# Output weights of a gated layer split into two parts where they are rounded, gate rows copied by one queue, last output products by token rows

## Chip, core and metric

The kernel runs on one core of a Trainium2 chip. The metric is the device time of one execution in microseconds (us); smaller is better. The core has five engines that work from their own instruction queues, in order: PE (TensorE, matrix products; PEld is its weight load), DVE (VectorE), ACT (ScalarE), POOL (GpSimd) and SP (SyncE, which only issues transfers). Transfers (DMAs) are issued from the queues of SP, ACT and POOL and carried by the same 16 DMA engines.

## The reference

```
X = rfft(x, axis=1);  y = irfft(X * (filt_r + 1j*filt_i))        # 8 batches, 3072 tokens, 256 wide
logits = y @ phi                                                 # 32 slots, 4 for each of 8 experts
slots  = softmax(logits over tokens).T @ y
slots  = relu(slots @ w1[e]) @ w2[e]                             # each expert on its own 4 slots
z = softmax(logits over slots) @ slots                           # back to 24576 tokens
out = (silu(z @ w_gate) * (z @ w_val)) @ w_out                   # 256 -> 1536 -> 256
```

## The kernel before

The work has three stages. **The first** (`phase1`) does the Fourier transforms as matrix products in 96 units, six for each of 16 half batches. A unit is written out by hand: load x (`load_x`, two transfers), products X with the transform (L258), multiplication by the filter on DVE and POOL (P, Q, yt), transposes T (L283) into a single buffer of PSUM, which ACT copies to `y` (L284), products with phi, and now and then a piece of the chain for the logits of an earlier batch (`chain`; its `dd` is computed by ACT at L428 and L435 and multiplied by PE at L443; its `lgd` are four transfers of logits to DRAM, L404).

Beside this runs a generator, `conv`, one step in the middle and one at the end of every unit. It rounds w_gate, w_val and w_out in 36 chunks of 128 x 256 numbers, chunks 24 to 35 being w_out. The four steps of a chunk are: ACT makes `mag` (L579); ACT makes `low` and the sign (L581, L582); DVE shifts `mag` (L584); POOL adds and multiplies into `low` (L586, L588), SP writes the result from `low` to DRAM (`wod` for w_out, L589) and loads the raw numbers (`raw`) of the chunk after next (L566). `mag`, `low` and `raw` have two buffers each, so chunk n+2 writes into the buffers of chunk n.

**The second** (`transition`) runs the experts on the 32 slots and multiplies the result by w_gate and w_val. So z never has to be formed: each token's 32 softmax weights times these rows (`g4`, `v4`, three tiles of 512 columns each) give gate and value. The rows are kept as a rounded part and the rest. Tile 0 is made in place; tiles 1 and 2 are copied there row by row with 16 transfers from `gh` and `gl` (L887), half of them on SP's queue and half on POOL's.

**The third** (`phase2`) goes over 576 items (batch, third, half, column block f of 12). For an item, `gv` makes G and V on PE (L980, L981) and silu on ACT (L983), `gate` the product h on DVE (L989), `split` a rounded part `hi` (ACT, L996) and the rest `lo` (DVE, L997), and three or four items later `proj` multiplies these by w_out on PE (L1008, L1012) into four accumulators, one for each block of 128 tokens (t). After the last f, ACT copies half of an accumulator (L1021), DVE adds the other half (L1022), and SP writes four transfers to `out`. w_out is loaded once in its second place (`wo`, index 1) by SP at the start of this stage, and `load_out` splits a block of it in each of the first twelve items: ACT rounds into index 0 (L969), POOL subtracts (L970).

Of the kernel before, what the change touches and what calls it, by code (L numbers as in the profile page):

```python
# [7 lines left out]
F32 = mybir.dt.float32  # L8
F32R = mybir.dt.float32r
# [3 lines left out]
ALU = mybir.AluOpType  # L13
# [4 lines left out]
NB, SEQ, D, E = 8, 3072, 256, 32  # L18
NEXP, SPE, FE, FF = 8, 4, 1024, 1536
NJ, NP, NR = 24, 96, 32  # L20
NF = FF // 128
# [58 lines left out]
def spectral_softmoe_glu_kernel(  # L80
# [17 lines left out]
    nc = tc.nc  # L98
    pe, dve, act, pool = nc.tensor, nc.vector, nc.scalar, nc.gpsimd

    dram = ctx.enter_context(tc.tile_pool(name="dram", bufs=1, space=DRAM))
# [8 lines left out]
    sb_ = const.tile([32, NB], F32, name="sb_")  # L110
    sp = const.tile([128, D], F32, name="sp")
    expo = const.tile([128, 1], F32, name="expo")
    wd = [dram.tile([256, FF], F32, name="wgd"), dram.tile([256, FF], F32, name="wvd"), dram.tile([FF, 256], F32, name="wod")]
    sld = dram.tile([128, NB - 2, D], F32, name="sld")
    cd = dram.tile([2, 3, E, 1024], F32, name="cd")
    lgd = [dram.tile([NP, 2, E, 16], F32, name=f"lgd{b}") for b in range(NB)]
# [20 lines left out]
    def phase1():  # L137
        with ExitStack() as c1:
# [412 lines left out]
            def flat(a):  # L551
                return a.rearrange("(p a) f -> p (a f)", p=128)

            def conv():


                cw = 256
                chunks = [(i, c) for i in range(3) for c in range(FF * D // 128 // cw)]
                raws = {}

                def load(n):
                    if n >= len(chunks):
                        return
                    i, c = chunks[n]
                    raws[n] = cvp.tile([128, cw, 2], I32, tag="raw", name="raw", bufs=2)
                    nc.sync.dma_start(  # L566
                        out=raws[n].rearrange("p n k -> p (n k)"),
                        in_=flat((w_gate, w_val, w_out)[i])[:, c * cw:(c + 1) * cw].bitcast(I32),
                    )

                load(0)
                load(1)
                yield
                for n, (i, c) in enumerate(chunks):
                    raw = raws.pop(n)
                    hf, lw = raw[:, :, 1].bitcast(F32), raw[:, :, 0].bitcast(U32)
                    mag = cvp.tile([128, cw], I32, tag="mag", name="mag", bufs=2)
                    low = cvp.tile([128, cw], I32, tag="low", name="low", bufs=2)
                    act.activation(mag.bitcast(F32), hf, AF.Copy, scale=2.0 ** -112)  # L579
                    yield  # L580
                    act.activation(low, lw, AF.Copy, scale=2.0 ** -29)  # L581
                    act.activation(hf, hf, AF.Sign)  # L582
                    yield
                    dve.tensor_scalar(mag, mag, 3, None, ALU.logical_shift_left)  # L584
                    yield
                    pool.tensor_tensor(out=low, in0=mag, in1=low, op=ALU.add)  # L586
                    mf = low.bitcast(F32)
                    pool.tensor_tensor(out=mf, in0=mf, in1=hf, op=ALU.mult)  # L588
                    nc.sync.dma_start(out=flat(wd[i])[:, c * cw:(c + 1) * cw], in_=mf)  # L589
                    load(n + 2)  # L590
                    yield

            def first_weights():

# [51 lines left out]
            for k in range(2):  # L646
# [4 lines left out]
                out=nyq, in_=bass.AP(filt_r.tensor, SEQ // 2 * D, [[1, 128], [128, 2]])  # L651
# [10 lines left out]
            todo = []  # L662
# [87 lines left out]
    def transition():  # L750
# [110 lines left out]
        for w, dst in gates:  # L861
            pg = bank([128, 512], "h")
            for d_ in range(2):
                pe.matmul(
                    out=pg, lhsT=sot[:, d_, :], rhs=w[:, d_, 0:512], start=(d_ == 0), stop=(d_ == 1)
# [7 lines left out]
        for d_ in range(2):  # L873
            for i, (w, n, c) in enumerate(parts):
                pe.matmul(
                    out=pg[32 * i:32 * i + 32, :],
                    lhsT=sot[:, d_, 0:32],
                    rhs=w[:, d_, c * 512:(c + 1) * 512],
                    start=(d_ == 0),
                    stop=(d_ == 1),  # L880
# [3 lines left out]
        dve.tensor_tensor(out=gl, in0=pg, in1=gh, op=ALU.subtract)  # L884
        for i, (w, n, c) in enumerate(parts):
            for r in range(4):
                (nc.sync if r < 2 else nc.gpsimd).dma_start(  # L887
                    out=later[n][c][32 * r:32 * r + 32, :].bitcast(F32),
                    in_=(gl if r % 2 else gh)[32 * i:32 * i + 32, :].bitcast(F32),
                )  # L890
# [4 lines left out]
    def phase2_tiles():  # L895
# [3 lines left out]
        wo4 = [cp.tile([128, 4, 2, D], F32R, name=f"wo{c}") for c in range(3)]  # L899
        wo = [wo4[f // 4][:, f % 4] for f in range(NF)]  # L900
        c4 = {}

        def first():
            t = cp.tile([128, 3, 2, 512], F32R, tag="c4", name="c4", bufs=2)

            for r in range(4):
                (nc.sync if r < 2 else nc.scalar).dma_start(
                    out=t[32 * r:32 * r + 32].rearrange("p q G n -> p q (G n)").bitcast(F32),
                    in_=cd[r // 2].rearrange("q e n -> e q n"),
                )  # L910
            c4[0] = t
            for c in range(3):
                nc.sync.dma_start(
                    out=wo4[c][:, :, 1, :].bitcast(F32),
                    in_=wd[2][c * 512:(c + 1) * 512, :].rearrange("(f p) d -> p f d", p=128),
                )

        def build(b):
# [42 lines left out]
    def phase2(later):  # L961
        cp, g4, v4, wo, c4, build = (later[k] for k in ("cp", "g4", "v4", "wo", "c4", "build"))
        kp = p2.enter_context(tc.tile_pool(name="kp", bufs=3))
        ps_g = p2.enter_context(tc.tile_pool(name="ps_g", bufs=2, space=PSUM))
        ps_o = p2.enter_context(tc.tile_pool(name="ps_o", bufs=1, space=PSUM))

        def load_out(f):
            st = wo[f][:, 1, :].bitcast(F32)
            act.copy(wo[f][:, 0, :], st)  # L969
            pool.tensor_tensor(out=wo[f][:, 1, :], in0=st, in1=wo[f][:, 0, :], op=ALU.subtract)  # L970

        items = [(b, q, G, f) for b in range(NB) for q in range(3) for G in range(2) for f in range(NF)]
        hb, hhi, hlo, acc, sb2 = {}, {}, {}, {}, {}

# [17 lines left out]
        def split(i):  # L992
# [4 lines left out]
            dve.tensor_tensor(out=lo, in0=h, in1=hi, op=ALU.subtract)  # L997
            hhi[i], hlo[i] = hi, lo

        def proj(i):  # L1000
            b, q, G, f = items[i]
            hi, lo = hhi.pop(i), hlo.pop(i)
            if f == 0:
                acc[0] = [ps_o.tile([128, 512], F32, tag=f"o{t}", name=f"o{t}") for t in range(4)]
            for t in range(4):
                a = acc[0][t]
                ts = slice(128 * t, 128 * t + 128)
                pe.matmul(  # L1008
                    out=a, lhsT=hi[:, ts], rhs=wo[f].rearrange("p k d -> p (k d)"),
                    start=(f == 0), stop=(f == NF - 1), skip_group_check=True,  # L1010
                )
                pe.matmul(  # L1012
                    out=a[:, D:2 * D], lhsT=lo[:, ts], rhs=wo[f][:, 0, :],
                    start=False, stop=(f == NF - 1), skip_group_check=True,
                )
            if f == NF - 1:
                ot = kp.tile([128, 4, D], F32, tag="ot", name="ot", bufs=2)
                for t in range(4):
                    a = acc[0][t]
                    tmp = kp.tile([128, D], F32, tag="tmp", name="tmp", bufs=4)  # L1020
                    act.copy(tmp, a[:, D:2 * D])  # L1021
                    dve.tensor_tensor(out=ot[:, t, :], in0=a[:, 0:D], in1=tmp, op=ALU.add)  # L1022
                row = b * SEQ + 1024 * q + 16 * G
                for ii in range(4):
                    nc.sync.dma_start(
                        out=bass.AP(out.tensor, (row + 4 * ii) * D, [[32 * D, 32], [1, 4 * D]]),
                        in_=ot[32 * ii:32 * ii + 32].rearrange("p t d -> p (t d)"),
                    )

        def lag(i):  # L1030

            r = i % (6 * NF) - EXP_AT
            if r in (1, 2, 3, 4, 5, 6):
                return (4, 3, 3, 3, 4, 4)[r - 1] if i < len(items) - 6 * NF else LAG
            return min(LAG, 3 + i // 10)

        todo = list(range(len(items)))
        gen = build(1)
        for i in range(len(items) + LAG):
            if i < len(items):  # L1040
                b, q, G, f = items[i]
                if q == 0 and G == 0 and f == 0 and b:
                    for _ in gen:
                        pass
                    gen = build(b + 1) if b + 1 < NB else iter(())
                gv(i)
            while todo and todo[0] <= i - lag(i):
                proj(todo.pop(0))
            if i < len(items):
                gate(i)  # L1050
            if i < NF:
                load_out(i)
            if 0 <= i - 1 < len(items):
                split(i - 1)
            if i % 4 == 1 and i > NF:
                next(gen, None)

    with tc.manual_schedule():
        phase1()
        phase2(transition())  # L1060
        p2.close()
# [32 lines left out]
```

## Time and profile before

| | |
|---|---|
| median of 3 runs (lowest to highest) | 1496.86 us (1495.06 to 1497.08) |
| the profiled execution: its time, its span | 1496.74 us, 1495.0 us |
| busy: PE, DVE, ACT, POOL | 96%, 78%, 64%, 16% of the span |
| chain that ended last, by engine | PE 85%, DVE 7%, DMA 3%, ACT 2% |
| first stage, second stage, third stage | to about 381, to about 407, to the end |

The span is that from the first to the last instruction of the profiled execution; 1.74 us of its time lie around it. "Busy" is time in which the engine executes. The chain that ended last is followed back from the last instruction, at each step to what released it.

### The profile page before, as it was taken

How to read it: one execution, taken by the hardware profiler on the slowest of the kernel's cores; microseconds unless marked ns; L12 is line 12 of the kernel's file. 1: busy time of each engine (PE TensorE's matmuls, PEld its weight loads, DVE VectorE, ACT ScalarE, POOL GpSimd, SP SyncE). 2: the span in 40 equal slices, each digit the busy share in tenths (PEclk: the TensorE clock that was granted, in tenths of full speed). 3: DMA queues.
4: the chain of work that ended last, by engine and by line, in shares of the span. 5: the costliest groups of instructions: out<-in, count | busy, mean ns of one | idle time of the engine just before them, and what ended most of it. 6: DMA issues, size and time to landing. Idle time of an engine off the chain costs nothing.

```text
span 1495.0 us, 25170 instructions
## 1 busy us (share of the span) xinstructions
PE 1440.3 (96%) x9562; PEld 1152.0 (77%) x9562; DVE 1163.0 (78%) x1894; ACT 961.1 (64%) x1837; POOL 243.5 (16%) x315
## 2 busy tenths in 40 slices
PE   4899899998899999999999999999999999999998
PEld 2566566665488888888888888888888888888887
DVE  2788888876378878878887887888789778877775
ACT  2476566663367667666766766676676667666665
POOL 0466666653020000000000000000000000000000
PEclk9999999999999999999999999999999999999999
DMA  9968877868710220220131112112110210211011
GB/s 226 156 118 160 154 131 148 167 153 339 277 44 14 51 60 15 50 60 16 28 71 27 27 36 54 36 29 48 48 29 20 66 39 23 49 43 25 19 29 29
DMA packets 87848, 116.42 MB, mean 78 GB/s; under 512 B 8880, under 2 KB 65072, under 8 KB 87600
## 3 DMA queue, kind: packets, MB, share of 16 engines
q1 hardware_dynamic: 80480, 102.37, 31.3%
q10 hardware_dynamic: 6800, 11.54, 2.5%
q8 instruction: 75, 1.23, 0.4%
q0 software_dynamic: 448, 0.92, 0.2%
q14 instruction: 45, 0.37, 0.1%
HBM read 68.13 MB, written 34.60 MB: 69 GB/s over the span
## 4 chain that ended last, share of the span: by engine, by line
PE 85%; DVE 7%; DMA 3%; ACT 2%; issue 1%; POOL 1%; SPq 0%; ACTq 0%; DVEq 0%; POOLq 0%
PE o L1008 35%; PE o L1012 18%; PE V L981 9%; PE G L980 9%; PE X L258 4%; PE s L230 2%; DVE sg L238 2%; PE T L283 2%; DVE P L262 1%; DVE Q L263 1%; PE c L477 1%; DMA fraw<-in_filt_i_dram 1%; PE L L291 1%; DMA raw<-in_moe_w_out_dram 1%; ACT b L247 1%
## 5 line engine op out<-in xcount | busy, mean ns | idle before, releaser
L1008 PE MATMUL o<-wo,hi 128*128 128x512 f32 x2304 | 833.1, 396 | 2.7 <-POOL wo L970 2.7
L1012 PE MATMUL o<-wo,lo 128*128 128x256 f32 x2304 | 645.3, 280 | 0.0
L983 ACT ACTIVATE s<-G 128x512 f32<-128x512 f32 x576 | 345.2, 599 | 322.7 <-PE G L980 319.4
L989 DVE TENSOR_TENSOR h<-V,s 128x512 f32<-128x512 f32 x576 | 395.0, 686 | 171.6 <-ACT s L983 170.8
L1008 PEld LDWEIGHTS o<-wo,hi 128*128 128x128 f32 x2304 | 432.9, 188 | 106.8 <-POOL wo L970 3.0
L1012 PEld LDWEIGHTS o<-wo,lo 128*128 128x128 f32 x2304 | 434.6, 189 | 25.3
L997 DVE TENSOR_TENSOR lo<-h,hi 128x512 fp32r<-128x512 f32 x576 | 422.4, 733 | 1.1
L996 ACT CAST hi<-h 128x512 fp32r<-128x512 f32 x576 | 354.7, 616 | 11.5 <-DVE h L989 8.2
L981 PE MATMUL V<-c,v 128*128 128x512 f32 x576 | 227.7, 395 | 1.1 <-DVE h L989 1.1
L980 PE MATMUL G<-c,g 128*128 128x512 f32 x576 | 228.3, 396 | 0.2 <-ACT s L983 0.2
L258 PEld LDWEIGHTS X<-fwd,b 128*128 128x128 f32 x768 | 95.6, 196 | 58.4 <-issue 41.0
L980 PEld LDWEIGHTS G<-c,g 128*128 128x128 f32 x576 | 108.2, 188 | 26.2 <-ACT s L983 0.9
L238 DVE STREAM_TRANSPOSE sg<-s 128x1024 f32<-128x1024 f32 x64 | 79.2, 1240 | 55.4 <-PE s L230 53.8
L258 PE MATMUL X<-fwd,b 128*128 128x128 f32 x768 | 112.0, 290 | 2.5 <-ACT b L247 1.3
L981 PEld LDWEIGHTS V<-c,v 128*128 128x128 f32 x576 | 108.7, 189 | 3.0 <-DVE h L989 2.4
L927 POOL TENSOR_TENSOR lg<-lg,mx 96x1024 f32<-96x1024 f32 x7 | 16.8, 2400 | 565.6 <-DVE mx L925 565.6
L247 ACT COPY b<-sg 128x768 f32<-128x768 f32 x64 | 58.7, 920 | 74.7 <-DVE sg L238 74.6
L1022 DVE TENSOR_TENSOR ot<-o,tmp 128x256 f32<-128x256 f32 x192 | 70.2, 424 | 39.6 <-ACT tmp L1021 39.6
L230 PE MATMUL s<-x,csm 48*64 48x512 f32 x512 | 73.1, 632 | 24.2 <-DMA x<-in_x_dram 16.9
L271 POOL TENSOR_TENSOR yt<-P 128x256 f32<-128x256 f32 x96 | 70.4, 733 | 118.1 <-DVE P L262 117.1
L262 DVE TENSOR_TENSOR P<-X,ft 128x512 f32<-128x512 f32 x96 | 64.1, 668 | 12.3 <-PE X L258 11.0
L273 POOL TENSOR_TENSOR yt<-Q 128x256 f32<-128x256 f32 x95 | 70.8, 745 | 0.4
(199 smaller groups left out, 982.2 us busy)
## 6 DMA issues: line engine op xcount, KB each, us to landing
out_dram<-ot SPq DMA_DIRECT2D x192, 128.0 KB, 2.2
x<-in_x_dram SPq DMA_DIRECT2D x60, 384.0 KB, 8.1
w<-in_moe_w_dram SPq DMA_DIRECT2D x8, 1024.0 KB, 11.1
w<-in_moe_w_dram ACTq DMA_DIRECT2D x13, 512.0 KB, 6.0
c<-ch SPq DMA_DIRECT2D x42, 128.0 KB, 2.3
c<-cl SPq DMA_DIRECT2D x42, 128.0 KB, 2.4
raw<-in_moe_w_gate_dram SPq DMA_DIRECT2D x12, 256.0 KB, 6.0
raw<-in_moe_w_val_dram SPq DMA_DIRECT2D x12, 256.0 KB, 4.3
```

The costliest lines, as they stand in the source:

```text
L230: pe.matmul(out=ps[64 * k:64 * k + 64, 16 * r:16 * r + 16, :], lhsT=s1t_sb[64 * r:64 * r + 48, :], rhs=xt[step][64 * r:64 * r + 48, k, :, ...
L238: dve.transpose(out=sg.rearrange("p j d k -> p d j k"), in_=ps.rearrange("p n d -> p d n"))
L258: pe.matmul(out=ps[:, g].rearrange("p r m -> p (r m)"), lhsT=bb[:, j, :], rhs=fwd[:, j, :])
L262: dve.tensor_tensor(out=P, in0=ps, in1=f, op=ALU.mult)
L980: pe.matmul(out=pg, lhsT=g4[c][:, fs], rhs=c4[b][:, q, G, :])
L981: pe.matmul(out=pv, lhsT=v4[c][:, fs], rhs=c4[b][:, q, G, :])
L983: act.activation(s, pg, AF.Silu)
L989: dve.tensor_tensor(out=h, in0=pv, in1=s, op=ALU.mult)
L996: act.copy(hi, h)
L997: dve.tensor_tensor(out=lo, in0=h, in1=hi, op=ALU.subtract)
L1008: pe.matmul(out=a, lhsT=hi[:, ts], rhs=wo[f].rearrange("p k d -> p (k d)"), start=(f == 0), stop=(f == NF - 1), skip_group_check=True,)
L1012: pe.matmul(out=a[:, D:2 * D], lhsT=lo[:, ts], rhs=wo[f][:, 0, :], start=False, stop=(f == NF - 1), skip_group_check=True,)
```

## The change

Three edits. (1) `conv` treats w_out differently: after POOL's product, the chunk is kept in `held`; one chunk later ACT rounds it into the `mag` tile (`high`), POOL subtracts (`rest`), and SP writes both parts to DRAM, whose tile `wod` is now twice as large. `first` loads both parts at once, and `load_out` is gone. (2) All 16 gate rows are copied by SP's queue. (3) The last two items are multiplied together, block of tokens by block of tokens (`close`), each block is evacuated when it is done, and the output leaves in eight transfers, four on SP's queue and four on ACT's.

```diff
+                halves = wd[2].rearrange("(p a) k f -> k p a f", p=128)
+                held = []
+                def high():
+                    for c, hi, mf in held:
+                        act.copy(hi, mf)
+                def rest():
+                    while held:
+                        c, hi, mf = held.pop()
+                        pool.tensor_tensor(out=mf.bitcast(F32R), in0=mf, in1=hi, op=ALU.subtract)
+                        for k, t in enumerate((hi.bitcast(F32), mf)):
+                            nc.sync.dma_start(out=halves[k, :, c], in_=t)
...
                     act.activation(mag.bitcast(F32), hf, AF.Copy, scale=2.0 ** -112)
+                    high()
                     yield
                     act.activation(low, lw, AF.Copy, scale=2.0 ** -29)
                     act.activation(hf, hf, AF.Sign)
+                    rest()
                     yield
...
-                    nc.sync.dma_start(out=flat(wd[i])[:, c * cw:(c + 1) * cw], in_=mf)
+                    if i == 2:
+                        held.append((c, mag.bitcast(F32R), mf))
+                    else:
+                        nc.sync.dma_start(out=flat(wd[i])[:, c * cw:(c + 1) * cw], in_=mf)
                     load(n + 2)
                     yield
+                high()
+                rest()
...
-                (nc.sync if r < 2 else nc.gpsimd).dma_start(
+                nc.sync.dma_start(
                     out=later[n][c][32 * r:32 * r + 32, :].bitcast(F32),
...
-                    out=wo4[c][:, :, 1, :].bitcast(F32),
-                    in_=wd[2][c * 512:(c + 1) * 512, :].rearrange("(f p) d -> p f d", p=128),
+                    out=wo4[c].rearrange("p f k d -> p f (k d)").bitcast(F32),
+                    in_=wd[2][c * 512:(c + 1) * 512].rearrange("(f p) k d -> p f (k d)", p=128),
...
-        def load_out(f):
-            st = wo[f][:, 1, :].bitcast(F32)
-            act.copy(wo[f][:, 0, :], st)
-            pool.tensor_tensor(out=wo[f][:, 1, :], in0=st, in1=wo[f][:, 0, :], op=ALU.subtract)
...
+        def close(two):
+            b, q, G, _ = items[two[0]]
+            ot = kp.tile([128, 4, D], F32, tag="ot", name="ot", bufs=2)
+            row = b * SEQ + 1024 * q + 16 * G
+            for t in range(4):
+                for i in two:
+                    part(i, t)
+                evac(ot, t)
+                if t % 2:
+                    for ii in range(4):
+                        (nc.scalar if ii % 2 else nc.sync).dma_start(
+                            out=bass.AP(out.tensor, (row + 4 * ii + t - 1) * D, [[32 * D, 32], [1, 2 * D]]),
+                            in_=ot[32 * ii:32 * ii + 32, t - 1:t + 1].rearrange("p t d -> p (t d)"),
+                        )
...
-        todo = list(range(len(items)))
+        todo = list(range(len(items) - 2))
...
+        close([len(items) - 2, len(items) - 1])
```

`part(i, t)` holds the two products of `proj` for one block of tokens, `evac(ot, t)` the copy and the addition; both are unchanged.

SP's queue in the first stage, at w_out's second and third chunk (chunks 25 and 26), before: `wod<-low` writes a chunk, `raw` is the load of the chunk after next, `cd` and `lgd` are the first batch's softmax weights and a batch's logits going to DRAM, `x` an input load.

```order
L589 DMA wod<-low 128x256
L566 DMA raw<-in_moe_w_out_dram 128x512
L636 DMA cd<-lgf 96x1024
L636 DMA cd<-ctf 96x1024
L178 DMA x<-in_x_dram 48x16x128 x2
L404 DMA lgd_75<-lg 48x512 x4
L589 DMA wod<-low 128x256
L566 DMA raw<-in_moe_w_out_dram 128x512
L178 DMA x<-in_x_dram 48x16x128 x2
```

The same place in the changed kernel, from the same load of `raw` on:

```order
L566 DMA raw<-in_moe_w_out_dram 128x512
L657 DMA cd<-lgf 96x1024
L657 DMA cd<-ctf 96x1024
L178 DMA x<-in_x_dram 48x16x128 x2
L404 DMA lgd_75<-lg 48x512 x4
L583 DMA wod<-mag 128x256
L583 DMA wod<-low 128x256
L566 DMA raw<-in_moe_w_out_dram 128x512
L178 DMA x<-in_x_dram 48x16x128 x2
```

Chunk 25 left first, ahead of the loads and the logits; now its two copies leave behind them, where chunk 26 stood. The same sequence comes once more, without `cd`, six chunks later (chunk 31).

ACT's queue at chunk 27 of the changed kernel, with what an instruction waits for behind it (DMAHW is a transfer's semaphore, the number its lane):

```order
L247 COPY b<-sg 128x24x32 [waits DVE_49]
L284 COPY y<-T 128x4x128 [waits PE_49]
L593 ACTIVATE mag<-raw 128x256 [waits DMAHW3_49,DMAHW2_49,Pool_49]
L576 CAST mag<-low 128x256 [waits Pool_49]
L428 ACTIVATE dd<-dd 128x512 [waits DVE_49] x2
L596 ACTIVATE low<-raw 128x256 [waits DMAHW4_49]
L597 ACTIVATE raw<-raw 128x256 [waits Activation_49]
L247 COPY b<-sg 128x24x32 [waits DVE_49]
L284 COPY y<-T 128x4x128 [waits PE_49]
L435 ACTIVATE dd<-dd 128x512 [waits Activation_49] x2
```

The instruction `mag` waited for one transfer before, the load of `raw`; now it waits for two, the second being the copy out of the buffer that it overwrites. `CAST mag<-low` is the new rounding of chunk 26; the rest stands as before.

## Rows read from the trace of the kernel before

**Rows 1.** Windows: us; busy of PE, PEld, DVE, ACT, POOL; granted clock; DMA share; GB/s.

```profile
285.00:325.00 40.00, 39.24 (x435) 25.45 (x434) 33.32 (x56) 27.56 (x57) 25.82 (x36) 1.00 0.90 174
...
413.00:420.00 7.00, 6.90 (x24) 5.80 (x25) 4.24 (x4) 2.12 (x5) 2.84 (x5) 0.62 0.39 95
...
460.00:960.00 500.00, 499.57 (x2679) 427.52 (x2678) 406.94 (x658) 348.38 (x644) 16.84 (x7) 1.00 0.17 41
```

**Rows 2.** Groups of instructions by line, `load_out`: busy us, mean ns, idle before.

```profile
L970 POOL TENSOR_TENSOR wo<-wo 128x256 fp32r<-128x256 f32 x12 | 8.7, 737 | 10.6 <-ACT wo L969 10.6
...
L969 ACT CAST wo<-wo 128x256 fp32r<-128x256 f32 x12 | 4.9, 406 | 0.0
```

**Rows 3.** Timeline of SP's queue, 256 to 266 us: start, duration of the issue.

```profile
258.85 0.38 SPq L566 DMA_DIRECT2D raw<-in_moe_w_out_dram  x1
...
260.29 2.58 SPq L178 DMA_DIRECT2D x<-in_x_dram  x2
262.99 2.42 SPq L404 DMA_DIRECT2D lgd<-lg  x4
265.51 0.94 SPq L589 DMA_DIRECT2D wod<-low  x1
```

**Rows 4.** Transfers issued at 257 to 259, 265.4 to 266.5, 305 us: KB, us to landing.

```profile
wod<-low SPq DMA_DIRECT2D x1, 128.0 KB, 1.7
...
wod<-low SPq DMA_DIRECT2D x1, 128.0 KB, 6.4
...
wod<-low SPq DMA_DIRECT2D x1, 128.0 KB, 6.2
```

**Rows 5.** Timeline of ACT at chunks 27 and 28: start, duration, idle before.

```profile
264.30 0.46 ACT L579 ACTIVATE mag<-raw 128x256 f32<-128x256 f32 x1
...
267.36 0.59 ACT L284 COPY y<-T 128x512 f32<-128x512 f32 x1
267.84 1.16 ACT L435 ACTIVATE dd<-dd 128x512 f32<-128x512 f32 x2
...
273.39 0.44 ACT L579 ACTIVATE mag<-raw 128x256 f32<-128x256 f32 x1 [1.82 <-DMA raw<-in_moe_w_out_dram]
```

**Rows 6.** Timeline of PE in the same stretch.

```profile
269.72 0.60 PE L283 MATMUL T<-csm,yt 128*128 128x128 f32 x4
...
270.25 1.09 PE L443 MATMUL c<-dd,csm 48*64 48x512 f32 x8
```

**Rows 7.** Timeline at chunk 33: SP, ACT and PE.

```profile
303.04 1.93 SPq L404 DMA_DIRECT2D lgd<-lg  x4
...
305.72 0.46 ACT L579 ACTIVATE mag<-raw 128x256 f32<-128x256 f32 x1
...
310.52 1.09 PE L443 MATMUL c<-dd,csm 48*64 48x512 f32 x8
```

**Rows 8.** All 36 chunks, by tile `low`: duration ns, first and last start us.

```profile
L581 ACT ACTIVATE low<-raw x36: 417/437/471, 79.3 to 321.2; 128x256 int32<-128x256 uint32 x36
```

**Rows 9.** Timeline at the start of the third stage, all engines.

```profile
409.99 0.69 DVE L997 TENSOR_TENSOR lo<-h,hi 128x512 fp32r<-128x512 f32 x1
...
412.39 0.79 SPq L887 DMA_DIRECT2D v<-gl  x1
...
413.10 0.80 PE L1008 MATMUL o<-wo,hi 128*128 128x512 f32 x1 [2.69 <-POOL wo L970]
...
416.26 0.63 PE L981 MATMUL V<-c,v 128*128 128x512 f32 x1
```

**Rows 10.** Tiles `v` and `wo` there: loads' issue and time to landing.

```profile
DMA to landing us min/median/max: 2.2/2.8/3.3
...
L913 SPq DMA_DIRECT2D wo<-wod x3: 439/759/1092, 391.5 to 393.2; - x3
DMA to landing us min/median/max: 8.9/11.1/11.4
```

**Rows 11.** Timeline at the end: SP's queue, the last four writes.

```profile
1490.49 1.72 SPq L1025 DMA_DIRECT2D out_dram<-ot  x4
```

More of the change, by code (lines that the diff above doesn't have):

```diff
@@ L112, in spectral_softmoe_glu_kernel @@
     expo = const.tile([128, 1], F32, name="expo")
-    wd = [dram.tile([256, FF], F32, name="wgd"), dram.tile([256, FF], F32, name="wvd"), dram.tile([FF, 256], F32, name="wod")]
+    wd = [dram.tile([256, FF], F32, name="wgd"), dram.tile([256, FF], F32, name="wvd"), dram.tile([FF, 2, 256], F32, name="wod")]
     sld = dram.tile([128, NB - 2, D], F32, name="sld")
@@ L998, in split, with part, evac @@
             hhi[i], hlo[i] = hi, lo
+        def part(i, t):
+            f = items[i][3]
+            a = acc[0][t]
+            ts = slice(128 * t, 128 * t + 128)
+            pe.matmul(
+                out=a, lhsT=hhi[i][:, ts], rhs=wo[f].rearrange("p k d -> p (k d)"),
+                start=(f == 0), stop=(f == NF - 1), skip_group_check=True,
+            )
+            pe.matmul(
+                out=a[:, D:2 * D], lhsT=hlo[i][:, ts], rhs=wo[f][:, 0, :],
+                start=False, stop=(f == NF - 1), skip_group_check=True,
+            )
+        def evac(ot, t):
+            a = acc[0][t]
+            tmp = kp.tile([128, D], F32, tag="tmp", name="tmp", bufs=4)
+            act.copy(tmp, a[:, D:2 * D])
+            dve.tensor_tensor(out=ot[:, t, :], in0=a[:, 0:D], in1=tmp, op=ALU.add)
+        def close(two):
[11 more added lines that the diff above has]
+                            in_=ot[32 * ii:32 * ii + 32, t - 1:t + 1].rearrange("p t d -> p (t d)"),
+                        )
         def proj(i):
             b, q, G, f = items[i]
-            hi, lo = hhi.pop(i), hlo.pop(i)
             if f == 0:
@@ L1005, in proj @@
             for t in range(4):
[L1006 to L1015, printed above, removed]
+                part(i, t)
+            hhi.pop(i)
+            hlo.pop(i)
             if f == NF - 1:
@@ L1018, in proj @@
                 for t in range(4):
[L1019 to L1022, printed above, removed]
+                    evac(ot, t)
                 row = b * SEQ + 1024 * q + 16 * G
@@ L1050, in phase2 @@
                 gate(i)
-            if i < NF:
-                load_out(i)
             if 0 <= i - 1 < len(items):
```

## The prediction

> **What bounds the kernel now.** I read the windows first, to see which engine each stage hangs on [rows 1]. In the third stage PE is busy 499.57 of 500 us: nothing gained on another engine there shortens anything, and an offset with which the stage begins is carried to the end. In the first stage, while w_out is rounded, PE is busy 39.24 of 40 us, so a pause forced on PE there has nearly nowhere to be caught up; ACT has 27.56 of 40 and POOL 25.82, so work added to them is mostly hidden, while a wait on them is not, since PE reads what ACT copies. Between the stages, the row 413 to 420 shows a granted clock of 0.62 (mostly the lower of the two levels, 1.2 GHz) after the pause of 2.69 us before the first output product [rows 9].
>
> Next I read the queues at the places where the change moves something: SP's queue where w_out is written [rows 3], how long those writes take to land [rows 4], what ACT and PE do there [rows 5, 6], and the two ends of the third stage [rows 9 to 11].
>
> **Edit 1, work added and removed.** Twelve roundings on ACT at 0.41 us and twelve subtractions on POOL at 0.74 us [rows 2] move from the start of the third stage to the first. In the third stage only those ahead of the first product were on the path. In the first stage they are 4.9 us of ACT and 8.8 us of POOL, spread over twelve chunks of (321.2 - 79.3) / 35 = 6.9 us each [rows 8]. The idle third of both engines covers most; bounds 0 and 4.9 us. I count them with the other copies below.
>
> **Edit 1, the new wait.** This is the term that decides. The `mag` of chunk n+2 overwrites the buffer from which SP copies the rounded part of chunk n, so ACT has to wait until that copy has landed. A chunk lasts 6.9 us, and the copy cannot leave before ACT has rounded, about 0.9 us into chunk n+1 (0.46 and 0.41): some 6 us are left. Whether that does depends on what stands ahead of the copy in SP's queue.
>
> At chunk 25 the new order puts two loads of x and four writes of logits ahead of it. In before this burst kept SP from 258.85 to 265.41 [rows 3], and the write of chunk 26, at 265.51, is where chunk 25's copies now stand; with one issue fewer ahead (some 0.4 us) the first leaves at 265.1. The write at 265.51 took 6.4 us to land, while one issued at 258 took 1.7 [rows 4]: the transfers of the burst are ahead of it on the DMA engines too. So the copy lands at about 265.1 + 6.4 = 271.5. ACT reaches `mag` of chunk 27 at 264.30 [rows 5] and stands for 7.2 us.
>
> Behind `mag` on ACT are the new rounding, two exponentials of the chain, the two conversions, the copy b and the copy y. In before y began 267.36 - 264.30 = 3.06 us after `mag`; now 0.41 later: 271.5 + 3.06 + 0.41 = 275.0, ended at 275.6. PE's next transpose T writes the one buffer that y empties, so it starts at about 275.7 instead of 269.72 [rows 6], 5.9 us late. PE's next product L443 needs ACT's second `dd`, 7.2 + 0.4 late: it ended at 267.84 + 1.16 = 269.0, will end at 276.6, and L443 starts at 276.7 instead of 270.25: **6.45 us late**. POOL's subtraction, which waits for ACT's rounding, and DVE's shift, which waits for `mag`, stand too, but both were ahead of PE. Part of this comes back: ACT waited 1.82 us for `raw` at 273.39 [rows 5], and that load will have landed. But the copy b behind it waits for DVE anyway, which is as late as PE; between 0 and 1.8 us, I take 0.25. **+6.2 us.**
>
> The burst comes again at chunk 31: the logits are issued from 303.04 until 304.97, the first copy leaves at about 304.65, and the write in that place took 6.2 us [rows 4, 7], so it lands at 310.85. `mag` of chunk 33 was reached at 305.72: ACT stands 5.1 us. PE's L443 began 4.80 us after that `mag`, with next to no slack behind ACT; it moves to 310.85 + 4.80 + 0.41 = 316.05, 5.5 us late. With 0.3 given back, **+5.2 us**.
>
> The other ten chunks have no such burst. Their copies have the 6 us; landing between 1.7 and 6.4, and after x loads at the long end, one or two wait up to 1.4. Together with the roundings that ACT cannot hide, bounds 0 and +6; **+1.0 us**.
>
> PE stands for 6 and 5 us in this, and the clock fell after 2.69 us of pause at the third stage. At 0.62 a row of 7 us loses 2.7 us [rows 1], so the bounds are 0 and +5.4 for both places; I take **+1.2 us**, nearer to nothing, since behind such a stall PE has to wait for ACT's and DVE's backlog anyway.
>
> **Edit 1 and 2, the start of the third stage.** The first output product waited until 413.10 for POOL, which issued its half of the gate rows and then subtracted. Now it needs `wo`, `hi` and `lo`; `lo` is made at 409.99 + 0.69 [rows 9], so it may start at about 410.8. `wo` is twice the bytes: issued from 391.5, 11.1 us to land, and even at double time it is there by 415 for the last of the three and well before for the first, which alone is needed [rows 10]; the gap up to the first product hides it, and without that gap PE would wait for the first third, one for one. But behind the first item's output products PE's queue holds G and V of item 4, which need tile 1 of `g4` and `v4`, and its eight copies of rows now all go through SP. SP's eighth issue was at 412.39 and takes 2.2 to 3.3 us to land, median 2.8 [rows 9, 10]: 415.2 to 415.7. V of item 4 began at 416.26 in before, so the 2.3 us won at the first product shrink to 0.6 to 1.1 us: the wait on POOL turns into one on the gate rows. I take **-0.7 us**. For the clock: PE still pauses some 3 us, only later, so I leave the low stretch as long as it was; if PE stays at 2.4 GHz, another 2 us are won; if the low stretch starts later and keeps its length, about 1 us is lost.
>
> **Edit 3.** The same products in another order. In before the last four writes were issued from 1490.49 to 1492.21, one after another, 0.43 us each [rows 11]. Now SP and ACT issue two each after the last block. But ACT's first two issues, after the second block, stand ahead of its copies of the third and fourth blocks, which then run one after the other: about 0.6 us later than PE would allow. Four issues become two, minus 0.86: **-0.2 us**, bounds -0.9 and +0.3.
>
> **The sum.** 6.2 + 5.2 + 1.0 + 1.2 - 0.7 - 0.2 = +12.7 us on the profiled execution's 1496.74, which is 0.12 below the median: 1509.4 us.
>
> **Rivals.** (A) *The copies overtake the burst.* In the trace a write behind it took 6.4 us, one with nothing ahead 1.7 [rows 4]; a copy of 128 KB might finish ahead of the logits' many small pieces. If it lands in 1.7 to 3.6 us, ACT stands about 2.5 to 4.5 and 0.6 to 2.5 us, PE is late by some 2 to 4 and 1 to 3; with the other terms at +1.0, 0, -0.7, -0.2, about +4, 1500.7 us. The Trainium skill, page "DMA: Bandwidth & Descriptors", section "Queues, rings and completion order", speaks for it in part: each DMA engine takes descriptors in ring order, but transfers need not complete in the order of issue; by that alone A would hold. The measured 6.4 and 6.2 us in this very place speak against it.
>
> (B) *PE catches up*, so it ends not slower. PE's ends are modelled, and the 39.24 of 40 us may hold hidden slack. If twelve units can be done 5 to 6 us faster after each stall, the first stage costs nothing and -0.9 is left: 1495.8 us, or 1493.8 if the clock also stays up. It decides from about 11 us of slack in 80 on. Against it: PE's products follow one another there with few gaps.
>
> (C) *More chunks wait.* Every landing of 6 us or more at another chunk stops ACT too, and a shifted first stage puts x loads in front of other copies. At 0.8 us for each of ten, +8: 1517 us.
>
> **Chances.** The forecast 0.60, A 0.15, B 0.15, C 0.10. The range reaches to A and to most of C, 1499 to 1516 us, and leaves out B and a third of C. Within 0.2% (3 us, about what this kernel's measurement tells from no change): a third of A and over half of B, 0.13; faster by more: the rest of B, 0.07; slower: 0.80. If the copies behave as forecast, the time is within 1504 to 1514.
>
> **What would show it.** In the changed kernel's trace: ACT's `mag` idle for some 7 us, and later 5, behind a transfer `wod<-mag`, at chunks 27 and 33; PE idle before T and L443 there; the first stage about 13 us longer; the first output product 2 to 3 us earlier after the gate products, and then a pause before V of item 4 behind `v<-gl`. I am wrong if `mag` does not wait there, if the copies land in under 4 us, or if PE's first stage is no longer than before although ACT stood.

## The result, and the profile after

| kernel | median | lowest to highest | runs | ratio to before, 95% interval |
|---|---|---|---|---|
| before | 1496.18 us | 1495.06 to 1497.08 | 4 | |
| changed | 1513.97 us | 1513.12 to 1515.2 | 4 | 1.0124 [1.0112, 1.0136] |
| changed, measured again in the last experiment | 1509.88 us | 1506.98 to 1514.17 | 6 | 1.0105 [1.0086, 1.0123] |
| before, beside that | 1494.97 us | 1492.03 to 1499.49 | 11 | |

Slower by 1.24% in the first measurement (17.8 us) and 1.05% in the second (14.9 us), where 0.8% (12.7 us, 1509.4 us) was forecast, and by the mechanism that was forecast. The profiled execution of the changed kernel took 1514.21 us, its span is 1512.4 us.

SP's queue in the changed kernel, where chunk 25's copies stand behind the burst (start, duration):

```profile
261.61 2.57 SPq L178 DMA_DIRECT2D x<-in_x_dram  x2
264.29 2.41 SPq L404 DMA_DIRECT2D lgd<-lg  x4
266.80 0.36 SPq L583 DMA_DIRECT2D wod<-mag  x1
```

ACT there (in brackets how long it stood before the instruction, and for what); the last row is `mag` of chunk 33:

```profile
265.63 0.58 ACT L284 COPY y<-T 128x512 f32<-128x512 f32 x1
272.99 0.43 ACT L593 ACTIVATE mag<-raw 128x256 f32<-128x256 f32 x1 [6.78 <-DMA wod<-mag]
...
276.11 0.57 ACT L284 COPY y<-T 128x512 f32<-128x512 f32 x1
...
319.81 0.43 ACT L593 ACTIVATE mag<-raw 128x256 f32<-128x256 f32 x1 [4.50 <-issue]
```

PE there, and at the second place:

```profile
269.38 1.16 PE L258 MATMUL X<-fwd,b 128*128 128x128 f32 x8
276.83 1.09 PE L283 MATMUL T<-csm,yt 128*128 128x128 f32 x4 [6.29 <-ACT y L284]
277.84 1.98 PE L443 MATMUL c<-dd,csm 48*64 48x512 f32 x8
...
282.99 1.50 PE L455 MATMUL c<-fwd,bd 128*32 128x128 f32 x48
...
323.65 1.09 PE L283 MATMUL T<-csm,yt 128*128 128x128 f32 x4 [4.01 <-ACT y L284]
324.67 1.98 PE L443 MATMUL c<-dd,csm 48*64 48x512 f32 x8
...
331.85 1.49 PE L455 MATMUL c<-fwd,bd 128*32 128x128 f32 x48
```

This is the chain of the prediction: the copy leaves at 266.80 and has landed by 272.99, 6.19 us later; ACT stands 6.78 us, `y` is late, PE's T stands 6.29 us. At chunk 33 ACT stands 4.50 us (the profile names no releaser; the copy left at 313.72 and by its own record took 6.0 us, so it landed just before) and PE 4.01. Forecast were 7.2 and 5.1 us for ACT. The reader should see a second thing: behind each pause T takes 1.09 us and L443 1.98, where they took 0.60 and 1.12 at full speed (shown with the first experiment). That is the lower of the two levels, 1.2 instead of 2.4 GHz, and it shows in the windows (the column after the five engines is the granted clock), where PE's busy time beside [rows 1] has fallen as well:

```profile
core 0: us, PE busy (x) PEld busy (x) DVE busy (x) ACT busy (x) POOL busy (x), PEclk, DMA share, GB/s
245.00:285.00 40.00, 32.11 (x331) 20.03 (x331) 30.64 (x49) 24.64 (x53) 22.96 (x33) 0.91 0.81 158
285.00:325.00 40.00, 34.60 (x355) 22.54 (x357) 28.70 (x48) 24.69 (x56) 27.16 (x39) 0.96 0.88 153
325.00:345.00 20.00, 19.31 (x208) 12.25 (x204) 11.16 (x19) 10.76 (x25) 11.26 (x16) 0.83 0.49 165
```

The start of the third stage on PE (gate rows rounded at 425.78; compare [rows 9]):

```profile
428.68 0.40 PE L1020 MATMUL o<-wo,hi 128*128 128x512 f32 x1
...
433.32 0.47 PE L997 MATMUL V<-c,v 128*128 128x512 f32 x1 [2.42 <-DMA v<-gl]
...
434.51 0.63 PE L1020 MATMUL o<-wo,hi 128*128 128x512 f32 x1
```

The first output product comes 2.90 us behind the rounding of the gate rows instead of 5.84, and then V of item 4 stands 2.42 us for the gate rows: the wait on POOL has become a wait on a queue, as forecast, and the clock falls behind it too (0.63 us for a row that takes 0.40).

**Where the difference of the spans lies.** ACT's copies `sl` (L493) come once for every six chunks and make marks. Starts in us; A is from the fourth to the fifth copy (chunks 24 to 29, with the wait at chunk 27), B from the fifth to the sixth (with the wait at chunk 33), C from there to the rounding of the gate rows `gh`, D from there to the end of the span. Names of the experiments are explained below.

| kernel | 4th `sl` | 5th | 6th | `gh` | span | A | B | C | D |
|---|---|---|---|---|---|---|---|---|---|
| before | 240.13 | 282.72 | 323.21 | 407.26 | 1495.0 | 42.6 | 40.5 | 84.0 | 1087.7 |
| changed | 241.96 | 291.22 | 340.07 | 425.78 | 1512.4 | 49.3 | 48.8 | 85.7 | 1086.6 |
| changed, again | 239.51 | 290.32 | 338.23 | 421.44 | 1506.5 | 50.8 | 47.9 | 83.2 | 1085.1 |
| spare buffers at 27 and 33 | 240.23 | 282.91 | 323.05 | 407.15 | 1492.9 | 42.7 | 40.1 | 84.1 | 1085.8 |
| spare at 27 | 241.01 | 283.92 | 331.61 | 414.80 | 1500.0 | 42.9 | 47.7 | 83.2 | 1085.2 |
| spare at 33 | 239.29 | 289.82 | 330.79 | 416.67 | 1503.3 | 50.5 | 41.0 | 85.9 | 1086.6 |
| copies by POOL's queue | 237.27 | 284.66 | 332.79 | 416.33 | 1501.1 | 47.4 | 48.1 | 83.5 | 1084.8 |
| x one unit later | 241.51 | 289.07 | 330.11 | 414.30 | 1499.7 | 47.6 | 41.0 | 84.2 | 1085.4 |
| logits by POOL's queue | 236.72 | 286.68 | 332.36 | 416.58 | 1502.5 | 50.0 | 45.7 | 84.2 | 1085.9 |
| long fill | 240.40 | 292.60 | 339.94 | 424.88 | 1511.6 | 52.2 | 47.3 | 84.9 | 1086.7 |
| short fill | 240.60 | 288.16 | 334.11 | 419.85 | 1506.5 | 47.6 | 46.0 | 85.7 | 1086.7 |
| edits 2 and 3 | 239.34 | 280.81 | 320.91 | 405.13 | 1491.5 | 41.5 | 40.1 | 84.2 | 1086.4 |
| spare, rows by two queues | 239.37 | 282.48 | 323.64 | 409.36 | 1492.3 | 43.1 | 41.2 | 85.7 | 1082.9 |
| the same, tail by POOL | 240.66 | 284.00 | 325.04 | 410.75 | 1493.9 | 43.3 | 41.0 | 85.7 | 1083.1 |

For the changed kernel: start +1.83, A +6.67, B +8.36, C +1.66, D -1.12, together the 17.4 us by which the spans differ.

### The profile page after: what moved, and what is told of

The parts are those of the page before. It is cut to its first block, busy times and chain, and to the rows that moved or that the text cites. A ratio compares the mean times of both kernels' runs of the same rounds, so it can differ in the third digit from the quotient of the medians.

```text
span 1512.4 us, 25187 instructions
## 1 busy us (share of the span) xinstructions
PE 1446.8 (96%) x9562; PEld 1155.2 (76%) x9562; DVE 1158.1 (77%) x1894; ACT 960.4 (64%) x1837; POOL 239.2 (16%) x307
## 4 chain that ended last, share of the span: by engine, by line
PE 85%; DVE 6%; DMA 4%; ACT 2%; issue 2%; POOL 1%; SPq 1%; ACTq 0%; DVEq 0%; POOLq 0%
PE o L1020 35%; PE o L1024 18%; PE V L997 9%; PE G L996 9%; PE X L258 4%; PE s L230 2%; PE T L283 2%; DVE sg L238 2%; DVE P L262 1%; DVE Q L263 1%; DMA fraw<-in_filt_i_dram 1%; PE c L477 1%; PE L L291 1%; DMA nyq<-in_filt_r_dram 1%; DMA lgf<-lgd 1%
## 5 line engine op out<-in xcount | busy, mean ns | idle before, releaser
L1024 PE MATMUL o<-wo,lo 128*128 128x256 f32 x2304 | 645.1, 280 | 0.0
L1024 PEld LDWEIGHTS o<-wo,lo 128*128 128x128 f32 x2304 | 434.2, 188 | 25.8 <-DVE lo L1013 0.5
L1032 ACT COPY tmp<-o 128x256 f32<-128x256 f32 x192 | 68.0, 374 | 4.9 <-PE o L1024 4.9
```

Source lines behind the costliest of these rows:

```text
L1024: pe.matmul(out=a[:, D:2 * D], lhsT=hlo[i][:, ts], rhs=wo[f][:, 0, :], start=False, stop=(f == NF - 1), skip_group_check=True,)
```

## The experiments

Theory: ACT's wait for two copies behind SP's burst, passed on to PE, is the cost. Rivals: the added roundings, subtractions and transfers cost by themselves; or the place on the queue is not what holds the copies.

**Spare buffers: both waits taken away, then one at a time.** Chunks 27 and 33 write into tiles that are idle then. The two buffers go on in turn behind them, so chunk 28 then writes where chunk 25 was, no longer where 26 was: its `mag` began at 272.69, while the copy of chunk 26, issued at 270.26, took 7.2 us to land. Everything else stays. For the single ones the condition is `n == 27` or `n == 33`.

```diff
+if n in (27, 33):
+    mag = sp.bitcast(I32)
+    low = yp[0].tile([128, cw], I32, tag="y1", name="low")
+else:
     mag = cvp.tile([128, cw], I32, tag="mag", name="mag", bufs=2)
     low = cvp.tile([128, cw], I32, tag="low", name="low", bufs=2)
```

Both: 

> The changed kernel, but chunks 27 and 33 get spare buffers for mag and low (a tile that is idle then), so ACT no longer has to wait for the copies of chunks 25 and 31 behind SP's burst; every copy and every rounding stays. Theory of the prediction (the two waits on the copies are what costs): ACT's idle time before mag of chunks 27 and 33 falls from 6.8 and 4.5 us to under 1 us, PE's pauses of 6.3 and 4.0 us before T go, the low clock after them goes too, and 13 to 15 of the 17.8 us come back: 1499 to 1502 us. Rival (the added roundings, subtractions and transfers cost by themselves, the waits only show it): at most half comes back, 1505 us or more.

Measured: 1496.53 us (10 runs), ratio 1.0009 [0.9999, 1.002]. ACT, then PE, at chunk 27 in this kernel:

```profile
264.38 0.44 ACT L597 ACTIVATE sp<-raw 128x256 f32<-128x256 f32 x1
264.72 0.39 ACT L576 CAST mag<-low 128x256 fp32r<-128x256 f32 x1
...
268.63 0.60 PE L283 MATMUL T<-csm,yt 128*128 128x128 f32 x4
269.16 1.12 PE L443 MATMUL c<-dd,csm 48*64 48x512 f32 x8
...
273.05 1.49 PE L455 MATMUL c<-fwd,bd 128*32 128x128 f32 x48
```

No wait, no pause, no slow row, and A and B are those of the kernel before (42.7 and 40.1). All but some 1 us of the loss came back, more than expected. The first rival falls: the twelve roundings, twelve subtractions and the twelve transfers more are not what costs. That they cost nothing is not shown: edits 2 and 3 without edit 1 (below) have a median 2.6 us lower, ten runs each, and 81.6 us in A and B where this kernel has 82.8.

Chunk 27 alone: 

> The changed kernel with a spare buffer at chunk 27 alone; chunk 33 still waits for the copy of chunk 31. Theory (two independent waits, each with its own price): the six chunks from 24 on are as in the kernel before, the six behind them stay as in the changed one, so 6 to 7 us come back: 1506 to 1509 us. Rival (the first wait only hides others, or the late first stage is what makes the second burst meet the copy): the wait moves to chunks 28 to 30 and under 3 us come back, or 12 us and more do.

Chunk 33 alone: 

> The changed kernel with a spare buffer at chunk 33 alone; chunk 27 still waits. Theory: 8 to 9 us come back (the second stretch of six chunks was 8.4 us longer, though ACT waited 4.5 us there, not 6.8): 1504 to 1507 us, and PE's granted clock stays at its upper level behind chunk 33. Rival (most of the 8.4 us is a late result of the first wait): under 4 us come back, over 1510 us.

Measured: 1502.32 us, 1.0053 [1.0037, 1.007], and 1502.3 us, 1.0052 [1.0036, 1.0067]. Each stretch is long exactly where its wait is left: A 42.9 and B 47.7, then A 50.5 and B 41.0. Both medians came lower than expected, since the expectations counted back from 1513.97 us. Seen from before, each kernel with one wait is 0.5% slower; together, less the 0.09% of the kernel without waits, that is 0.96%, inside the interval of the repeated measurement, though under that of the first. With the stretches this says that the two waits add up.

**What holds the copies.** Three kernels, each with one line of the changed kernel edited: copies by POOL's queue, x one unit later, logits by POOL's queue.

```diff
-nc.sync.dma_start(out=halves[k, :, c], in_=t)
+nc.gpsimd.dma_start(out=halves[k, :, c], in_=t)
...
-if u in (0, 2):
+if u in (1, 3):
     load_x(s + 2, u // 2)
...
-(nc.gpsimd if last else nc.sync).dma_start(
+nc.gpsimd.dma_start(
     out=lgd[b]
```

Copies by POOL's queue: 

> The changed kernel, but the rounded part and the remainder are copied by POOL's queue instead of SP's, so they do not stand behind the loads of x and the logits. Theory (place in SP's queue, the issue at 266.8 us and what is ahead of it there): the copies of chunk 25 leave about 4 us earlier and land in 2 to 3 us, ACT waits under 1 us, 1499 to 1503 us. Rival (the DMA engines are busy with the burst whichever queue it is): landing stays at 5 us or more, ACT still waits 2 to 4 us at chunks 27 and 33, 1504 to 1510 us.

Measured: 1504.98 us, 1.0072 [1.0052, 1.0091]. POOL issues at chunk 25, and ACT at chunk 27:

```profile
258.40 0.57 POOL L583 DMA_DIRECT2D wod<-mag  x1
...
264.86 0.43 ACT L593 ACTIVATE mag<-raw 128x256 f32<-128x256 f32 x1 [3.33 <-issue]
```

Counted from the fourth `sl`, the copy left 3.7 us earlier than on SP's queue (21.1 us behind it instead of 24.8), and still ACT went on only 6.46 us after it, about as long as on SP's queue (6.19). The expected 2 to 3 us were wrong; the rival had it: another queue did not shorten the landing. The Trainium skill, page "DMA: Bandwidth & Descriptors", section "Queues, rings and completion order", says that each DMA engine takes turns between the queues that have work for it; the trace agrees in so far as the copy landed ahead of the second load of x, which was issued just before it on SP's queue and took 9.1 us; at chunk 31 (issued at 305.37, 8.0 us) it landed behind both loads. What the earlier issue gave is the smaller wait at chunk 27 (3.33 instead of 6.78): there the place in SP's queue alone is worth 3.45 us of the wait. Another 3.42 us came at chunk 28, behind the next copy, and at chunk 33 ACT stood 4.92 us, no less than in the changed kernel (4.50).

X one unit later: 

> The changed kernel, with every later load of x issued one unit (3.4 us) later: units 1 and 3 of six instead of 0 and 2. In SP's queue the loads of x then stand behind the copies of chunks 25 and 31; the four writes of logits stay ahead of them. No buffer is added. Theory (it is mostly the bytes of x that the copies wait behind on the DMA engines): the copies land in 2 to 4 us, ACT waits under 1.5 us at chunks 27 and 33, 1497 to 1502 us. Rival 1 (the logits' many small pieces hold the copies): ACT still waits over 3 us there, 1506 us or more. Rival 2 (x comes too late for its transform): PE waits for x at each step, slower than the changed kernel.

Measured: 1502.38 us, 1.0051 [1.0036, 1.0067]. SP's queue, now with the loads of x behind the copy, and ACT at chunks 27 and 28:

```profile
261.15 3.46 SPq L404 DMA_DIRECT2D lgd<-lg  x4
265.03 0.34 SPq L583 DMA_DIRECT2D wod<-mag  x1
265.49 0.36 SPq L583 DMA_DIRECT2D wod<-low  x1
265.94 1.04 SPq L178 DMA_DIRECT2D x<-in_x_dram  x2
...
267.48 0.44 ACT L593 ACTIVATE mag<-raw 128x256 f32<-128x256 f32 x1 [1.72 <-POOL yt L273]
...
276.00 0.45 ACT L593 ACTIVATE mag<-raw 128x256 f32<-128x256 f32 x1 [2.48 <-DMA wod<-mag]
```

With the logits and not x ahead, the copy landed in 2.4 us. ACT still stood 1.72 us for it: the profile names POOL, but that instruction had ended at 266.99, and the copy landed at 267.4. B is cured (41.0). A is not (47.6): the loads of x now stand ahead of the next copies, and ACT waits 2.48 and 2.40 us at chunks 28 and 29. The mechanism came out as the theory had it, the time just above its upper end (1502): moving the loads moved part of the wait.

Logits by POOL's queue: 

> The changed kernel, with all writes of logits issued by POOL's queue; the loads of x stay ahead of the copies on SP's queue. Theory (it is x's bytes that the copies wait behind): the copies of chunks 25 and 31 leave some 2.4 us sooner but land only as the loads of x let them, ACT still waits 3.5 us or more at chunks 27 and 33, 1507 to 1513 us. Rival (the four issues and small pieces of the logits are the larger part): ACT waits under 2 us, 1497 to 1503 us.

Measured: 1505.43 us, 1.006 [1.0036, 1.0083], under the expected range, though with the expected wait. SP's queue and ACT:

```profile
256.36 2.56 SPq L178 DMA_DIRECT2D x<-in_x_dram  x2
259.01 0.74 SPq L583 DMA_DIRECT2D wod<-mag  x1
...
267.36 0.43 ACT L593 ACTIVATE mag<-raw 128x256 f32<-128x256 f32 x1 [6.64 <-DMA wod<-mag]
```

The copy left early, right behind the loads of x, and took 8.35 us; ACT stood as long as in the changed kernel. At chunk 33 it stood 3.65 us; the profile names POOL, but the copy, issued at 305.83, took 8.3 us and landed just before. The logits were in flight here too, on POOL's queue. The case of x without logits stands in the changed kernel itself, at the copy of chunk 28, for which `mag` of chunk 30 waited:

```profile
286.90 0.95 SPq L178 DMA_DIRECT2D x<-in_x_dram  x2
287.95 0.48 SPq L583 DMA_DIRECT2D wod<-mag  x1
...
296.69 0.45 ACT L593 ACTIVATE mag<-raw 128x256 f32<-128x256 f32 x1 [1.75 <-issue]
```

It took 8.7 us to land, the last logits having been issued 21 us before; chunk 27's copy, issued at 280.43 when the loads of x had landed, took 1.7. Together, in these places: with x ahead or beside 6.2 to 8.7 us, without x at most 2.5. It is x's transfers that the copies wait behind; the burst made it worse by holding back the issue.

**The clock.** Products that nobody reads fill PE's two pauses (13 and 8 in the long fill, 6 and 4 in the short one); ACT's waits stay.

```diff
+if i in (CONV_AT + 56, CONV_AT + 68):
+    dummy = ps_l.tile([128, 512], F32, tag="L", name="dummy")
+    for j in range(13 if i == CONV_AT + 56 else 8):
+        pe.matmul(out=dummy, lhsT=ident, rhs=fwd[:, 0:4, :], start=True, stop=True)
 tail_ops(i)
```

Long fill: 

> The changed kernel, and PE is given 13 and 8 products whose result nobody reads (identity by resident filter columns, 128x512), placed just before the two transposes at which it stands for 6.3 and 4.0 us; ACT's waits stay. Theory (of the 15 us of the first stage some 5.5 are the lower clock behind the two pauses, by the rows 1.7 and 3.8 us): with PE at work the clock stays up, T to L455 takes 4.4 us instead of 6.2 and 8.2, and 3 to 5.5 us come back though PE has more work: 1508.5 to 1511 us. Rival (the slow rows cost nothing, since PE waits there for ACT's and DVE's backlog): within 1.5 us of the changed kernel, or slower by what the products take beyond the pause, 1512.5 to 1516 us.

Short fill: 

> As the kernel with unread products in PE's two pauses, but 6 and 4 of them: one takes 0.86 us, so the 13 and 8 of the first try took 11.3 and 7.0 us, 5 and 3 us more than the pauses; 6 and 4 take 5.2 and 3.4 us and fit. Theory (the slow rows behind the pauses are part of the price): the clock stays up, T to L455 takes 4.4 us as with the long fill, and the sum of both stretches falls from 98.1 to some 93 us: 1508 to 1511 us. Rival (what the clock gives is lost again in waits for ACT and DVE): 97 us or more, 1512.5 us or more.

Measured: 1512.22 us, 1.0113 [1.0096, 1.0131], with the long fill, and 1506.51 us, 1.0058 [1.0038, 1.0078], with the short one. PE with the long fill, then with the short one:

```profile
268.82 11.32 PE L728 MATMUL dummy<-fwd,csm 128*128 128x512 f32 x26
279.98 0.60 PE L283 MATMUL T<-csm,yt 128*128 128x128 f32 x4
280.51 1.09 PE L443 MATMUL c<-dd,csm 48*64 48x512 f32 x8
```

```profile
269.02 5.32 PE L728 MATMUL dummy<-fwd,csm 128*128 128x512 f32 x12
275.12 0.63 PE L283 MATMUL T<-csm,yt 128*128 128x128 f32 x4 [0.78 <-ACT y L284]
...
279.93 1.50 PE L455 MATMUL c<-fwd,bd 128*32 128x128 f32 x48
```

The long fill was mis-sized: 13 products (two records each) took 11.32 us where the pause was 6.3, and its time fell between the ranges of theory and rival. But T and L443 are back at 0.60 and 1.09 us. With the short fill from T to L455 it is 4.81 us, against 6.16 and 8.20 in the changed kernel (276.83 to 282.99, 323.65 to 331.85) and 4.42 without waits (268.63 to 273.05), and A and B together are 93.5 us instead of 98.1, as expected; the granted clock is 1.00 in all three windows from 245 to 345 us. The median came under the expected 1508 to 1511 us. A kernel in which PE does more work is faster, since the work fell where PE would have stood: the lower clock is 4.6 of the 15.0 us that A and B lost; the other 10.4 are what is left with both waits in place.

**The two ends of the third stage.** Edits 2 and 3 alone, with the output weights split at the start of the third stage as before: 

> Edits 2 and 3 alone: gate rows by SP's queue and the last two units by token rows, while the output weights are loaded whole and split by ACT and POOL at the start of the third stage as in the kernel before. Theory: the first stage is that of before to within 0.5 us; POOL reaches its subtraction sooner, so the first output product starts 1 to 2 us earlier, and V of item 4 then waits for the gate rows; with the tail minus 0.4 this is 0.5 to 1.5 us under before, 1495 to 1496 us. Rival (edit 2 costs as much as it gives, or the clock falls deeper at the start of the third stage): 1496.5 to 1498 us.

Measured: 1493.97 us, 0.9993 [0.998, 1.0006]; in the profile D is 1.4 us shorter than before, V of item 4 stands 1.92 us for the gate rows. The median cannot be told from before. The first output product starts 2.99 us behind the rounding of the gate rows (408.12), more of a gain than expected and as much as in the changed kernel (2.90), though the split is still made in the third stage: edit 2 alone brings it. So what edit 1 takes out of the third stage gives nothing there that edit 2 does not, and D is the same with and without it (1086.4 and 1086.6).

Spare buffers, and the gate rows by two queues again (`nc.sync if r < 2 else nc.gpsimd`): 

> As the kernel with spare buffers at chunks 27 and 33, and half of the gate rows issued by POOL's queue again (edit 2 undone). POOL has no subtraction there any more, so it holds nothing up. Theory (V of item 4 waits 2.4 us for the eighth of eight issues on one queue): the last row lands some 1.5 us sooner, and the third stage starts 1 to 1.7 us earlier than with one queue: 1 to 1.7 us under the kernel with spare buffers. Rival (the pause is filled by the low clock or by another operand): within 0.5 us of it.

Measured: 1493.16 us, 0.9986 [0.9973, 0.9999]; that is 3.4 us under the kernel with spare buffers alone, more than expected. V of item 4 with one queue (spare buffers alone), then with two:

```profile
414.67 0.47 PE L1001 MATMUL V<-c,v 128*128 128x512 f32 x1 [2.41 <-DMA v<-gl]
```

```profile
414.83 0.47 PE L1001 MATMUL V<-c,v 128*128 128x512 f32 x1 [0.46 <-DMA v<-gl]
```

The wait shrank by 1.95 us, D by 2.8 (1085.8 to 1082.9). Slow rows went with it: behind the pause of 2.41 us L1024 takes 0.63 us in a row of products, behind 0.46 us it stays at 0.39. So edit 2 gave away part of what edit 1 won here: once POOL has no subtraction, its queue is free for half of the rows. Even so the kernel is not shown to be faster than edits 2 and 3 alone (1493.16 against 1493.97 us).

The same, with the last writes by SP and POOL instead of SP and ACT: 

> Spare buffers at chunks 27 and 33, half of the gate rows by POOL's queue, and the last writes of token rows by SP and POOL instead of SP and ACT, so that ACT's copies of the last two blocks do not stand behind its own writes. Theory: those two copies start some 0.6 to 1 us sooner and the span ends 0.5 to 0.9 us sooner than with ACT's queue; 1491.5 to 1493.5 us, 1.5 to 3.5 us under the kernel before. Rival (POOL's issues land later than ACT's): the end is where it was, 1493 to 1495 us.

Measured over 12 runs: 1493.62 us, 0.998 [0.997, 0.999], 3.0 us under before. ACT's last copies no longer wait, but from the end of PE's last product to the end of the span it is 5.2 us (1488.69 to 1493.9) against 5.0 in the run before it (1487.26 to 1492.3): the rival was right, in this profile POOL's queue gives nothing at the end.

**The changed kernel once more.** 

> The changed kernel once more, unaltered. In its first profile 1.83 us were lost before chunk 24, where the change does nothing, and 1.66 us between the last of the waits and the gate rows; spare buffers at one chunk alone gave 11.7 us each by their medians, 23.4 together, where both at once gave 17.5. Theory (these two parts are chance of an execution): the fourth copy sl comes at 237 to 241 us, not at 241.96, the two stretches of six chunks are again 14 to 16 us longer than in before, and the median is 1510 to 1513 us. Rival (they belong to the change): the start is late again by 1.5 to 2 us, and the median is 1513.5 to 1515 us.

Measured: 1509.88 us, 1.0105 [1.0086, 1.0123], just under the theory's range (1510 to 1513). The fourth `sl` came at 239.51; A and B lost 15.6 us (15.0 the first time), C was even shorter than before. So 3.5 us of the first profile (start and C) were not the change's.

## Why the prediction was right

By its own steps:

- **The wait at chunk 25's copy, +6.2.** Right in place, cause and size. Forecast landing 6.4 us, measured 6.19; ACT 7.2, measured 6.78 (6.90 the second time); T 5.9 late, stood 6.29 (5.27).
- **The wait at chunk 31's copy, +5.2.** Right in place and cause: landing 6.1 us (313.72 to 319.81), ACT 4.50 and 4.69 against 5.1. A little too large: PE stood 4.01 and 4.20.
- **Other ten copies and the roundings, +1.0.** Small, and not told apart from the forecast or from nothing: with both waits gone, A and B together are 82.8 to 84.4 us in three kernels, against 83.1 before and 81.6 with edits 2 and 3 alone.
- **The clock behind the stalls, +1.2, bounds 0 and 5.4.** This term was mis-sized: the short fill shows 4.6 us, 5.2 against the repeat. The reason given, that PE waits for ACT's and DVE's backlog behind a stall anyway, failed: with ACT held up as before, PE kept at work ran T to L455 in 4.81 us. The mean of 0.62 in [rows 1] pointed to 2.7 us for each pause; that bound was the better value.
- **Start of the third stage, -0.7, and tail, -0.2.** Shape right; D was 1.1 and 2.7 us shorter in the two profiles. The tail gave about 0.4: from the end of PE's last product to the end of the span 5.0 us instead of 5.4. The first part was put down to edits 1 and 2 together; edit 2 alone does it. The forecast left the low stretch as long as it was.
- **Rivals.** A (the copies overtake the burst) is refuted by the landings of 6.2 to 8.7 us with x's transfers in flight; it would have held behind the logits alone. That an order is not assured does not mean that it is broken, so "by that alone A would hold" went too far; and A's own terms come to +3.1 to +7.1, not about +4. B (PE catches up): the short fill still loses 10.4 us in A and B where 11.4 of waits were forecast, so 1 to 2 us at most are caught up. C (more chunks wait): a few waits of 0.7 to 1.8 us at other chunks, not 0.8 at each of ten.

The sum with the clock at 4.6 instead of 1.2 is +16.1, between the two measured differences of 17.8 and 14.9. How close it comes is in part luck: the start and C together are 4.9 us apart in the two profiles, and the mis-sized term is covered by the width of the range. What stays open: why the start of the program took 1.8 us longer in all that the first profile of the changed kernel shows ahead of chunk 24, where its instructions are those of before.

## What to carry to other kernels

A two-deep buffer whose contents are written out by a transfer is freed not by the issue but by the landing, so price the landing behind whatever else is in flight, at the worst place in the schedule, and give those places a third buffer. Moving a small copy to another queue helped here by its earlier issue alone, at one of the two places and not at the other, since the bytes of x were in flight whichever queue it was. Price a pause of PE of some microseconds together with the slow rows behind it: here that was nearly half as much again.

## What was not expected of the hardware

- Another queue did not shorten a landing: 6.46 us from POOL's, 6.19 from SP's; without x ahead, from SP's, at most 2.45.
- PE given 8.9 us of unread products (5.32 and 3.60) made the kernel 3 to 7 us faster (1506.51 us against 1509.88 and 1513.97).
- The same mark, the fourth `sl`, lies anywhere from 237.27 to 241.96 us in the twelve profiles of kernels whose instructions before it are the same (all but x one unit later and logits by POOL's queue); and C is 83.2 to 84.9 us or 85.7 to 85.9. In all five kernels with the longer C the granted clock is 0.91 to 0.94 from 345 to 365 us, in the changed kernel as in two without the waits at chunks 27 and 33. Four runs of one kernel can agree within 2 us and still be 4 us off its next median.
